# A decode-attention kernel that streams 162 MB: keys scored 16384 at a time, values in 64-column tiles, a row-form mixer, and a new division of the load buffers

## The chip, the cores and the metric

The kernel runs on one core of one Trainium2 chip. The metric is the device time of one execution in microseconds (us), median over several runs. The runs of the kernel before agree within 0.2%.

The words used below: PE is the matrix engine, PEld its weight loads, DVE the vector engine, ACT the scalar engine, SP the engine that issues the loads. "The queue" is the one DMA queue on which SP issues every large load; it is worked off by 16 DMA engines in parallel. A DMA engine moves one row of a load, here mostly 32 KB, as one packet.

## The reference, cut to what matters

One token is decoded. Attention has 32 query heads on 4 key/value heads, 65536 cached positions of 128 elements; beside it stands a small gated mixer, and a sigmoid gate blends the two.

```python
# per kv head g: K, V are [65536, 128] bf16 (16.8 MB each); 8 query heads share them
q      = x @ wq                                   # wq  1024 x 4096   (8.4 MB)
p      = softmax(q @ K.T * 128**-0.5)
a      = concat_heads(p @ V) @ wo                 # wo  4096 x 1024   (8.4 MB)
z      = gelu(x @ w_in)                           # w_in 1024 x 3584  (7.3 MB)
b      = (z[:1792] * (w_sp * layernorm(z[1792:]) + b_sp)) @ w_out   # w_out (3.7 MB)
gate   = sigmoid((x * gate_w).sum())
out    = gate * a + (1 - gate) * b
```

Every byte is read once: 162 MB for hardly any arithmetic. All keys of a head must be scored before its values are used, because the maximum is taken first.

## The kernel before

A recorder notes each operation with what it reads and writes; each engine runs its own operations in the order in which they were recorded and waits on semaphores where an operand comes from another engine or a load. Loads are issued in one fixed order, and a load waits until the readers of the buffer that it overwrites are done. If that wait lasts longer than the loads already queued, the queue runs dry.

```python
NS, SLOT = 5, 16384            # ring of five slots, 128 partitions x 32 KB = 4 MB each

def k_piece(n, j):             # a quarter of 8192 keys
    P("DVE", lambda e: e.transpose(ktb(i).bitcast(F32), sl[:, 2048*j:2048*(j+1)].bitcast(F32)),
      r=[key], w=[("kt", i % NKTS)])                     # three buffers for transposed keys
    def f(e):
        for fe in range(4):
            ins = e.matmul(pf(sb), qpad[g % 2][:, o:o+128], vw(ktb(i), ...),   # 128 x 512, own weight load
                           start=(j == 0 and fe == 0), stop=(j == 3 and fe == 3))
    P("PE", f, r=[("qpad", g % 2), ("kt", i % NKTS)], w=[B(sb)])
    ...
def pv_piece(n):               # 8192 values: 16 matmuls, four column tiles of 32
    for b in range(16):
        cg = b % 4
        ins = e.matmul(pf(OB)[32*cg:32*(cg+1), :], ptsb(n)[:, 32*b:32*(b+1)], vw(sl, 128*b, [[2048,4],[1,128]]),
                       tile_position=(0, 32*cg), ...)
def win_piece(i):              # mixer in column form: 4 x 56 matmuls with one column each
    for k in range(2):
        for z in range(2*FC):
            ins = e.matmul(pf(MB)[:, z:z+1], vw(sl, c0, [[FC,128]]), xT[:, 2*i+k:2*i+k+1], ...)
# ... (softmax, mixer's small operations, output product cut)
```

## Time and profile before

| | before |
|---|---|
| median | 386.56 us (3 runs, 386.56 to 386.72) |
| span in the profile | 384.9 us |
| moved by the queue | 162.01 MB |
| PE, DVE busy | 61%, 55% |
| DMA engines busy with packets | 98.2% |

The lines below are from the page of the kernel before: span, busy time of the engines, the rate of the queue in 40 equal slices, the queue's total with its share of 16 engines' span, and the shares of the chain that ended last.

```profile
span 384.9 us, 3607 instructions
PE 233.6 (61%) x1547; PEld 86.2 (22%) x1547; DVE 211.6 (55%) x329; ACT 30.6 (8%) x71; POOL 2.1 (1%) x9
...
GB/s 331 436 433 440 430 424 437 429 435 433 427 433 426 427 433 429 433 432 436 433 429 436 424 429 436 429 431 430 433 433 431 433 430 429 434 433 422 421 418 169
...
q1 hardware_dynamic: 6200, 162.01, 98.2%
...
DMA 71%; PE 16%; DVE 11%; issue 0%; SPq 0%
```

The row counts a packet in the slice where it starts, so it wavers by some 10 GB/s without any idle time; only a clear drop outside the two ends would be time in which the queue had nothing to do, and before, there is none. The share of 98.2% says the same.

The costliest groups of the page of before (line, engine, operation, shapes, count | busy us, mean ns of one | idle before, and who ended it):

```profile
L472 PE MATMUL pb<-arena 128*128 128x512 bf16 x512 | 160.0, 457 | 93.6 <-DVE arena L464 91.7
L464 DVE STREAM_TRANSPOSE arena<-arena 128x1024 f32<-128x1024 f32 x128 | 151.4, 1217 | 75.3 <-DMA arena<-in_A_k_cache_dram 75.0
L472 PEld LDWEIGHTS pb<-arena 128*128 128x128 bf16 x512 | 46.7, 109 | 201.3 <-DVE arena L464 144.9
L516 PE MATMUL pb<-arena 128*32 128x512 bf16 x512 | 39.3, 441 | 20.6 <-DMA arena<-in_A_v_cache_dram 18.1
...
L558 PE MATMUL pb<-arena 128*128 128x1 bf16 x224 | 13.7, 198 | 0.0
```

Key matmuls wait for DVE's transposes, and those wait for the load of the keys (75 us): this chain of waits leads back to the queue.

### The profile page before, as it was taken

To read this page: it belongs to the slowest core of one execution; us is meant where nothing else is said; L and a number is where in the kernel's file an instruction comes from. 1 tells how busy PE (TensorE), PEld (TensorE's weight loads), DVE (VectorE), ACT (ScalarE), POOL (GpSimd) and SP (SyncE) were. 2 spreads that over 40 slices of the span, in tenths; PEclk is the share of its full clock that TensorE was granted. 3 is DMA by queue.
4 is the path that set the end of the run, shared out by engine and by line. 5 is a ranking of instruction groups with operands and counts; after the bars stand their busy time and mean duration, and the time that the engine had idled before them with its cause. 6 is when DMAs were issued, how large, how long until landed. Compare 5 with 4: busy or idle time off the path is not lost.

```text
span 384.9 us, 3607 instructions
## 1 busy us (share of the span) xinstructions
PE 233.6 (61%) x1547; PEld 86.2 (22%) x1547; DVE 211.6 (55%) x329; ACT 30.6 (8%) x71; POOL 2.1 (1%) x9
## 2 busy tenths in 40 slices
PE   0434888478776656563687574726983829533354
PEld 0111455423221111111222121212220202211121
DVE  4115454489967474655596656645974748511010
ACT  1000000100300000001010000000100000320000
POOL 2000000000000000000000000000000000000000
PEclk9985969569996969696889696956796979866655
DMA  8999999999999999999999999999999999999994
GB/s 331 436 433 440 430 424 437 429 435 433 427 433 426 427 433 429 433 432 436 433 429 436 424 429 436 429 431 430 433 433 431 433 430 429 434 433 422 421 418 169
DMA packets 6228, 162.24 MB, mean 422 GB/s; under 512 B 700, under 2 KB 708, under 8 KB 964
## 3 DMA queue, kind: packets, MB, share of 16 engines
q1 hardware_dynamic: 6200, 162.01, 98.2%
q8 instruction: 12, 0.20, 0.2%
q14 instruction: 4, 0.03, 0.0%
q10 hardware_dynamic: 12, 0.00, 0.0%
HBM read 162.01 MB, written 0.00 MB: 421 GB/s over the span
## 4 chain that ended last, share of the span: by engine, by line
DMA 71%; PE 16%; DVE 11%; issue 0%; SPq 0%
DMA arena<-in_A_k_cache_dram 59%; PE pb L472 11%; DMA arena<-in_A_v_cache_dram 10%; DVE arena L464 9%; DMA arena<-in_A_wo_dram 3%; PE pb L516 2%; PE pb L558 2%; DVE arena L485 1%; PE pb L650 1%; DVE arena L507 0%; DVE arena L533 0%; PE pb L538 0%; PE pb L528 0%; SPq L349 0%; PE pb L495 0%
## 5 line engine op out<-in xcount | busy, mean ns | idle before, releaser
L472 PE MATMUL pb<-arena 128*128 128x512 bf16 x512 | 160.0, 457 | 93.6 <-DVE arena L464 91.7
L464 DVE STREAM_TRANSPOSE arena<-arena 128x1024 f32<-128x1024 f32 x128 | 151.4, 1217 | 75.3 <-DMA arena<-in_A_k_cache_dram 75.0
L472 PEld LDWEIGHTS pb<-arena 128*128 128x128 bf16 x512 | 46.7, 109 | 201.3 <-DVE arena L464 144.9
L516 PE MATMUL pb<-arena 128*32 128x512 bf16 x512 | 39.3, 441 | 20.6 <-DMA arena<-in_A_v_cache_dram 18.1
L502 ACT ACTIVATE arena<-arena 128x512 bf16<-128x512 f32 x32 | 23.1, 720 | 224.0 <-DVE arena L507 171.1
L507 DVE STREAM_TRANSPOSE arena<-arena 128x512 bf16<-128x512 bf16 x32 | 21.6, 679 | 18.5 <-PE pb L516 18.5
L485 DVE TENSOR_SCALAR_CACHE_REDUCE arena<-pb 128x512 f32<-128x512 f32 x32 | 21.6, 674 | 8.1 <-PE pb L472 7.9
L516 PEld LDWEIGHTS pb<-arena 128*32 128x32 bf16 x512 | 12.8, 106 | 45.0 <-issue 37.1
L558 PEld LDWEIGHTS pb<-arena 128*128 128x128 bf16 x224 | 13.8, 161 | 0.4
L558 PE MATMUL pb<-arena 128*128 128x1 bf16 x224 | 13.7, 198 | 0.0
L650 PE MATMUL pb<-arena 128*1 128x256 bf16 x128 | 7.8, 410 | 6.3 <-DMA arena<-in_A_wo_dram 6.3
L530 DVE RECIPROCAL arena<-pb 128x1 f32<-128x1 f32 x4 | 0.7, 168 | 18.4 <-PE pb L528 18.4
L419 PE MATMUL pb<-arena 128*2 128x512 bf16 x64 | 6.8, 601 | 4.2 <-DMA arena<-in_A_wq_dram 4.2
L656 DVE TENSOR_TENSOR arena<-pb,arena 97x256 bf16<-97x256 f32 x1 | 0.4, 425 | 13.4 <-PE pb L650 13.4
L396 PE MATMUL pb<-arena 1*128 1x2 bf16 x1 | 0.2, 158 | 10.1 <-DMA arena<-in_B_b_sp_dram 10.1
L426 DVE CAST arena<-pb 98x512 bf16<-98x512 f32 x1 | 0.7, 692 | 10.2 <-PE pb L419 10.2
L502 ACT ACTIVATION_READ_ACCUMULATOR arena<-arena 128x1 f32 x32 | 6.0, 187 | 0.0
L650 PEld LDWEIGHTS pb<-arena 128*1 128x1 bf16 x128 | 3.4, 109 | 10.5 <-DMA arena<-in_A_wo_dram 7.6
L538 PE MATMUL pb<-arena 128*128 128x128 bf16 x16 | 1.8, 243 | 5.2 <-DVE arena L533 5.2
L573 ACT ACTIVATE arena<-arena 128x28 f32<-128x28 f32 x1 | 0.2, 227 | 55.8 <-DVE arena L572 55.8
L569 DVE COPY arena<-pb 128x28 f32<-128x28 f32 x1 | 0.2, 186 | 7.8 <-PE pb L558 7.8
L398 DVE COPY arena<-pb 128x2 f32<-128x2 f32 x1 | 0.2, 159 | 7.7 <-PE pb L396 7.7
(88 smaller groups left out, 50.4 us busy)
## 6 DMA issues: line engine op xcount, KB each, us to landing
arena<-in_A_k_cache_dram SPq DMA_DIRECT2D x16, 4096.0 KB, 30.9
arena<-in_A_v_cache_dram SPq DMA_DIRECT2D x16, 4096.0 KB, 36.4
arena<-in_A_wq_dram SPq DMA_DIRECT2D x2, 4096.0 KB, 17.2
arena<-in_B_w_in_dram SPq DMA_DIRECT2D x2, 3584.0 KB, 40.9
arena<-in_A_wo_dram SPq DMA_DIRECT2D x3, 2048.0 KB, 34.9
arena<-in_B_w_out_dram SPq DMA_DIRECT2D x1, 3584.0 KB, 34.4
arena<-in_A_wo_dram SPq DMA_DIRECT2D x1, 1024.0 KB, 23.1
arena<-in_A_wo_dram SPq DMA_DIRECT2D x2, 512.0 KB, 13.1
```

The lines of the kernel that those rows point to most:

```text
L419: ins = e.matmul(pf(OB)[32 * cg:32 * cg + 2, :], xw[:, 3 * c + 1 - s:3 * c + 3 - s], sl[:, WQ_N * k + 512 * (4 * s + cg):WQ_N * k + 512 * ...
L426: P("DVE", lambda e: e.tensor_copy(qsb[0:98, :], pf(OB)[0:98, :]), w=[("psb", 0), B(OB)])
L464: P("DVE", lambda e: e.transpose(ktb(i).bitcast(F32), sl[:, 2048 * j:2048 * (j + 1)].bitcast(F32)), r=[key], w=[("kt", i % NKTS)])
L472: ins = e.matmul(pf(sb), qpad[g % 2][:, o:o + 128], vw(ktb(i), 64 * f2 + ev, [[128, 16], [2, 32]]), start=(j == 0 and fe == 0), stop=(j == ...
L485: P("DVE", lambda e: e.tensor_scalar(scs(n), pf(sb), 0.0, None, op0=ALU.add, op1=ALU.max, accum_out=maxc[:, n:n + 1]), w=[("sc", n % NSC), ...
L502: P("ACT", lambda e: e.activation(psb(n), scs(n), ACTF.Exp, bias=gcol(g, K_NB), scale=SCALE, accum_out=lp[:, n:n + 1]), r=[("sc", n % NSC) ...
L507: P("DVE", lambda e: e.transpose(ptsb(n), psb(n)), r=[("psb", n % 2)], w=[("ptsb", n % 2)])
L516: ins = e.matmul(pf(OB)[32 * cg:32 * (cg + 1), :], ptsb(n)[:, 32 * b:32 * (b + 1)], vw(sl, 128 * b, [[2048, 4], [1, 128]]), start=(u == 0 ...
L530: P("DVE", lambda e: e.reciprocal(gcol(g, K_RL), pf(MB)[:, 0:1]), w=[("rl", g), B(MB)])
L538: ins = e.matmul(pf(MB)[:, 0:128], sel[:, 128 * c:128 * (c + 1)], osc[:, 128 * c:128 * (c + 1)], start=(c == 0), stop=(c == 3))
L558: ins = e.matmul(pf(MB)[:, z:z + 1], vw(sl, c0, [[FC, 128]]), xT[:, 2 * i + k:2 * i + k + 1], start=(i == 0 and k == 0 and z == 0), stop=( ...
L650: ins = e.matmul(pf(FB)[32 * q:32 * q + 1, 0:QW], ovec[:, 8 * i + c:8 * i + c + 1], sl[:, o:o + QW], start=(i == 0 and c == 0), stop=(i == ...
```

## The change

The intent is to feed PE in larger pieces. A query weight is loaded once and used for two PSUM banks, so 16384 keys are scored per step; values go through two column tiles of 64 with shared weights; the mixer's input product is turned so that x is the weight and w_in streams in rows of 448 columns. The 20 MB of load buffers are divided anew: three 4 MB slots for keys (and a few weights), and one 8 MB region for values, wq, w_in and most of wo (the last two value blocks go to key slots). The core of the diff, with cuts:

```diff
-    NS = 5
-    SLOT = 16384
+    SUB = 16384
+    KR = 3                       # key ring: 3 slots of 4 MB
+    NSUB = KR + 2                # and an 8 MB value region behind it
-    NKTS = 3
+    NKT = 2
 ...
+    def mm(e, loaded, *a, **kw):             # a matmul that reuses the weights already loaded
+        if not loaded:
+            return e.matmul(*a, **kw)
+        ...  dataclasses.replace(one, ..., ldweights=False)
 ... # order of the loads
+    load([("wq", 0)], rows(A_wq, 0, 8), VB)
+    load_k(0)
+    load_k(1)
+    load([("win", 0)], rows(B_w_in, 0, 8), VB)
+    load_k(2)
+    load_k(3)
+    load([("wout", 0)], rows(B_w_out, 0, 14), kring())
+    for i in range(6):
+        load_k(2 * i + 4)
+        load_v2(2 * i)                       # two value blocks, the whole region
+        load_k(2 * i + 5)
+    load_v2(12)
 ... # a load is cut into DMAs of one slot, each waiting only for the readers of its own part
+            for c in range(0, w, SUB):
+                m = min(SUB, w - c)
+                P("SP", ... e.dma_start(arena[:, o:o + m], src), w=[("slot", x) for x in grains(off + c, m)], ...)
 ... # key scoring
-                ins = e.matmul(pf(sb), qpad[g % 2][:, o:o + 128], vw(ktb(i), 64 * f2 + ev, [[128, 16], [2, 32]]), ...)
+                for b in range(2):
+                    ins = mm(e, b > 0, sc_ps(n)[:, 512 * b:512 * (b + 1)], qpad[:, o:o + 128],
+                                   vw(ktb(i), 2048 * b + 64 * f2 + ev, [[128, 16], [2, 32]]), ...)
 ... # values
+            for i in range(16):
+                b, t, cg = i // 8, 2 * (i % 8), i % 2
+                for h in range(2):
+                    ins = mm(e, h > 0, ob[64 * cg:64 * (cg + 1), 512 * h:512 * (h + 1)], ..., tile_position=(0, 64 * cg))
 ... # mixer
+            for c in range(KC):
+                for k in range(4):
+                    for s in range(2):
+                        ins = mm(e, s > 0, ob[32 * k:32 * k + 1, 512 * s:512 * s + FB4], xT[:, c:c + 1], sl[:, o:o + FB4],
+                                       tile_position=(0, 32 * k), ...)
 ... # the order at the start
+    k_step(0)
+    k_step(1, evac=0, own=True)
+    mixer_piece()
+    k_step(2)
+    k_step(3, evac=2)
+    wout_piece()
```

## The prediction

> **What bounds the kernel now.** The DMA queue. The slices row shows 424 to 440 GB/s in all slices but the first (331) and the last four (422, 421, 418, 169). The queue moved 162.01 MB; at 432 GB/s that is 375 us of the 384.9 us span. The Trainium skill, "DMA: Bandwidth & Descriptors", Specifications, puts the fabric ceiling at 435 GB/s; this trace agrees (about 431 held). The rest is about 3 us before data flows and, after the last weights land at 381.7 us (chain of waits), some PE and DVE work and the store. PE (233.6 us, 61%) and DVE (211.6 us, 55%) have slack. The chain is 71% DMA.
>
> **What the change does.** The bytes stay, in rows of 32 KB as before.
> - Keys: 512 matmuls stay, their 512 weight loads (46.7 us, mostly overlapped) become 256. 128 transposes of 1.22 us become 64 of an estimated 2.35; 32 evictions of 0.67 become 16 of about 1.25. Saves about 5 us of DVE.
> - Values: 512 matmuls stay, but two column tiles run side by side instead of four. Before, 16 took 1.01 us (timeline); I estimate 2 us per 16 warm, 3.4 cold: PE gains 30 us of work.
> - Mixer: 224 one-column matmuls (13.7 us) become 64 of 448 columns, about 7 us, plus 2.2 us of row copy and transpose on DVE.
> - Buffers: still 20 MB, but keys own three 4 MB slots and values one 8 MB region that isn't double buffered.
>
> None of the saved engine time lies on the critical path. The change can win almost nothing; it loses where the queue runs dry.
>
> **Where the queue could run dry** (estimates from the trace's durations; a 4 MB load takes 9.7 us).
> 1. The fifth key load reuses the slot of key block 2, whose transposes stand on DVE behind the mixer. w_in lands at about 59.4, its matmuls end at 67.5, copy and transpose take 2.2, the small operations 6.0 (70.7 to 76.7 before), and block 2's transposes, paced by a cold PE (0.39 to 0.43 us per matmul), end at about 87.5. The queue has drained by about 86.3. Gap 2.5 us, range 0 to 6.
> 2. Values 12-13 wait for the product of block 11, with only one 9.7 us key load between instead of two. Gap 1 us, range 0 to 4.
> In the steady state the products end some 14 us before the region is needed: no gap. The tail is the same.
>
> **Predicted: 388.8 us**, range 385.6 to 394.0. Faster by over 2%: 0.02 (it would need a DMA rate above 435). Within 2%: 0.88. Slower by over 2%: 0.10.
>
> **What would show each step.** Right: DMA about 71% or more of the chain; steady slices at 425 to 440 GB/s; one slice near 85 to 95 us down to 300 to 400, with the fifth key load's issue waiting for block 2's last transpose; perhaps a smaller dip near 320 us, waiting for a value product. Groups: transposes near 2.35 us, 256 key weight loads, value products 2 to 3.4 us per 16. The skill's "TensorE: Matmul & The Clock Gate", Part 1, has an idle PE at half rate; the trace agrees (16 key matmuls at 34 us took 6.28 us, later ones 0.26 each).
> Wrong: no dip at all (then about 386), or dips every 39 us.
>
> **What would make it wrong.** Two matmuls sharing a weight in one column tile may not overlap the other tile: products of 7 to 14 us per block, and gap 2 grows to 6 us. Key and value rows now stand 64 KB apart in HBM; if that lowers the rate by 1%, it costs 4 us.

## The result, and the profile after

| | before | after |
|---|---|---|
| median | 386.64 us (4 runs, 386.56 to 386.75) | 386.15 us (4 runs, 385.93 to 386.49) |
| ratio | | 0.9988, 95% interval 0.9974 to 1.0002 |
| span in the profile | 384.9 us | 384.5 us |

A ratio is the mean time of one kernel's fast runs over that of the other's in the same rounds, so it isn't quite the ratio of the medians quoted beside it. The change is within the noise of nothing: the predicted loss of 2.2 us (388.8 against 386.6) did not come.

The same lines of the page of after:

```profile
span 384.5 us, 2520 instructions
PE 236.3 (61%) x1367; PEld 57.8 (15%) x777; DVE 212.3 (55%) x229; ACT 25.8 (7%) x42; POOL 1.5 (0%) x8
...
GB/s 328 436 436 436 435 417 440 433 403 419 435 426 426 423 436 431 436 436 433 433 431 433 433 436 421 426 426 430 436 436 428 433 436 433 429 433 424 418 424 204
...
q1 hardware_dynamic: 6200, 162.01, 98.4%
...
DMA 63%; PE 18%; DVE 17%; SPq 1%; issue 1%; ACT 0%
```

The ninth slice (76.9 to 86.5 us) shows 403 and the tenth 419: the predicted dip is there, but shallow. The 417 of the sixth slice is no gap: the packet records have no idle time in it. Everywhere else the queue is as full as before. Three in ten of the instructions are gone (3607 to 2520), and it made no difference. The chain's DMA share fell from 71% to 63% although the queue is busy for 98.4% of the span, against 98.2%: more of the chain runs through DVE (17% against 11%) and PE (18% against 16%). The faster kernel of run 2 has only 55% DMA in it, so this share is no measure of how bound the kernel is.

The groups of after that answer to those of before:

```profile
L483 DVE STREAM_TRANSPOSE arena<-arena 128x2048 f32<-128x2048 f32 x64 | 145.2, 2292 | 81.9 <-DMA arena<-in_A_k_cache_dram 73.6
L253 PE MATMUL scp<-arena 128*128 128x512 bf16 x256 | 108.7, 425 | 85.4 <-DVE arena L483 62.0
L255 PE MATMUL scp<-arena 128*128 128x512 bf16 x256 | 107.7, 421 | 0.0
...
L253 PEld LDWEIGHTS scp<-arena 128*128 128x128 bf16 x256 | 26.9, 105 | 190.7 <-DVE arena L483 95.8
```

L253 and L255 are the first and second matmul of a shared weight; their spans overlap, so their busy times must not be added. Key weight loads went from 46.7 to 26.9 us and key transposes from 151.4 to 145.2 us, and DVE waits for the keys' load as long as before (73.6 against 75.0 us). Nothing of this reached the time. DVE's total didn't fall either (211.6 before, 212.3 after): the mixer's copy and transpose add 2.2 us, a second pass over each head's output 2.9 us and smaller operations about 3 us; the rest is overlap of neighbouring records, which the total counts once.

**Where the queue came closest to running dry.** First the timeline of DVE in after (start, duration, what, and in brackets the idle time before it with its releaser). L595 takes the mixer's sums out of PSUM, L625 is the mixer's last operation, L483 are the transposes of key block 2, which stand behind the mixer; the cut leaves out the mixer's small operations.

```profile
66.46 1.09 DVE L595 COPY arena<-obt 128x896 f32<-128x896 f32 x1 [10.27 <-PE obt L255]
67.58 1.11 DVE L597 STREAM_TRANSPOSE arena<-arena 128x896 f32<-128x896 f32 x1
...
74.47 0.23 DVE L625 SCALAR_TENSOR_TENSOR arena<-arena 128x14 bf16<-128x14 f32 x1
74.62 4.50 DVE L483 STREAM_TRANSPOSE arena<-arena 128x2048 f32<-128x2048 f32 x2
80.61 2.31 DVE L483 STREAM_TRANSPOSE arena<-arena 128x2048 f32<-128x2048 f32 x1 [1.50 <-PE scp L255]
83.58 4.50 DVE L483 STREAM_TRANSPOSE arena<-arena 128x2048 f32<-128x2048 f32 x2 [0.66 <-PE scp L255]
```

Block 2's last transpose is the first of the two that begin at 83.58, so it ends at about 85.9. The issue of the fifth key load follows at once, in the timeline of SP:

```profile
85.92 0.33 SPq L373 DMA_DIRECT2D arena<-in_A_k_cache_dram  x1
```

The packet records of the trace give the rest. The last packets of w_out end between 86.37 and 87.87 us, engine by engine, and the first packet of the fifth key load starts at 86.87. So the engines that were ahead stood idle for up to about a microsecond, and the hindmost not at all: 0.47 us averaged over the 16. The Trainium skill, "DMA: Bandwidth & Descriptors", Specifications, gives 0.6 us as the first-byte latency of a load issued from SP; here it is 0.62 us from the end of the issue (86.25) to the first packet.

**The packets right after such a gap are slow.** Packets of 32 KB take 1.220 us on average in the profile of before. The 17 slow ones just after the gap took 0.53 us more per engine in total, as the first ones of the whole program do (0.54 us in the first 10 us). So this gap cost its idle time and about half a microsecond to start again. Slow packets alone are no sign of a gap: the same profile has 27 of them between 36 and 49 us (0.25 us per engine) with no idle time of note.

### The profile page after: what moved, and what is told of

It is laid out like the page before. It is cut to its first block, busy times and chain, and to the rows that moved or that the text cites. A ratio compares the mean times of both kernels' runs of the same rounds, so it can differ in the third digit from the quotient of the medians.

```text
span 384.5 us, 2520 instructions
## 1 busy us (share of the span) xinstructions
PE 236.3 (61%) x1367; PEld 57.8 (15%) x777; DVE 212.3 (55%) x229; ACT 25.8 (7%) x42; POOL 1.5 (0%) x8
## 3 DMA queue, kind: packets, MB, share of 16 engines
q1 hardware_dynamic: 6200, 162.01, 98.4%
## 4 chain that ended last, share of the span: by engine, by line
DMA 63%; PE 18%; DVE 17%; SPq 1%; issue 1%; ACT 0%
DMA arena<-in_A_k_cache_dram 33%; DVE arena L483 11%; DMA arena<-in_A_v_cache_dram 8%; DMA arena<-in_B_w_in_dram 8%; DMA arena<-in_A_wo_dram 8%; DMA arena<-in_A_wq_dram 6%; PE obt L253 5%; PE obt L255 5%; PE scp L253 4%; PE scp L255 3%; SPq L373 1%; DVE arena L500 1%; DVE arena L521 1%; DVE arena L556 0%; DVE arena L471 0%
## 5 line engine op out<-in xcount | busy, mean ns | idle before, releaser
L483 DVE STREAM_TRANSPOSE arena<-arena 128x2048 f32<-128x2048 f32 x64 | 145.2, 2292 | 81.9 <-DMA arena<-in_A_k_cache_dram 73.6
L253 PE MATMUL scp<-arena 128*128 128x512 bf16 x256 | 108.7, 425 | 85.4 <-DVE arena L483 62.0
L255 PE MATMUL scp<-arena 128*128 128x512 bf16 x256 | 107.7, 421 | 0.0
L253 PE MATMUL obt<-arena 128*64 128x512 bf16 (+2 forms) x334 | 70.1, 445 | 31.5 <-DMA arena<-in_A_v_cache_dram 15.2
L255 PE MATMUL obt<-arena 128*64 128x512 bf16 (+2 forms) x334 | 69.7, 442 | 0.0
L253 PEld LDWEIGHTS scp<-arena 128*128 128x128 bf16 x256 | 26.9, 105 | 190.7 <-DVE arena L483 95.8
L253 PEld LDWEIGHTS obt<-arena 128*64 128x64 bf16 (+1 forms) x334 | 20.8, 118 | 92.7 <-issue 88.1
L516 ACT ACTIVATE arena<-arena 128x1024 bf16<-128x1024 f32 x16 | 18.4, 1148 | 223.3 <-DVE arena L512 112.5
L500 DVE TENSOR_SCALAR_CACHE_REDUCE arena<-scp 128x1024 f32<-128x1024 f32 x16 | 19.3, 1205 | 9.3 <-PE scp L255 9.3
L521 DVE STREAM_TRANSPOSE arena<-arena 128x1024 bf16<-128x1024 bf16 x16 | 19.4, 1213 | 8.1 <-PE obt L255 5.5
L706 PE MATMUL fbt<-arena 128*1 128x256 bf16 x128 | 7.0, 384 | 4.2 <-DMA arena<-in_A_wo_dram 4.1
L595 DVE COPY arena<-obt 128x896 f32<-128x896 f32 x1 | 1.1, 1091 | 10.3 <-PE obt L255 10.3
L706 PEld LDWEIGHTS fbt<-arena 128*1 128x1 bf16 x128 | 3.4, 106 | 7.5 <-DMA arena<-in_A_wo_dram 4.6
```

What stands on the lines that cost most here:

```text
L253: return e.matmul(*a, **kw)
L255: one = e.matmul(*a, **kw).ins
L483: P("DVE", lambda e: e.transpose(ktb(i).bitcast(F32), sl[:, 4096 * p:4096 * (p + 1)].bitcast(F32)), r=keys[2 * p:2 * p + 2], w=[("kt", i % ...
L500: P("DVE", lambda e: e.tensor_scalar(scs(n), sc_ps(n), 0.0, None, op0=ALU.add, op1=ALU.max, accum_out=maxc[:, n:n + 1]), w=[("sc", n % NSC ...
L516: P("ACT", lambda e: e.activation(psb, scs(n), ACTF.Exp, bias=gcol(n // NP, K_NB), scale=SCALE, accum_out=lp[:, n:n + 1]), r=[("sc", n % N ...
L521: P("DVE", lambda e: e.transpose(ptsb(n), psb), r=["psb"], w=[("ptsb", n % 2)])
```

## The experiments

The averages of idle and slow time that follow come from the packet records of each profile, between 78 and 98 us: idle is time with fewer than 16 packets in flight, divided over the 16 engines; slow is the excess of packets over 1.3 us above 1.220 us, also per engine.

### 1. The changed kernel again, as yardstick

> The changed kernel again, as the yardstick for the three runs beside it and as a second profile of it. Expected 386.0 to 386.5 us, 0.1% under the kernel before. In the packets of the DMA queue the only gap in the middle is again at 86 to 88 us, about 0.5 us averaged over the 16 engines; the engines' last packets end within about 2 to 4 us of each other, and this spread at the end differs from run to run.

Measured: 386.04 us (6 runs, 385.34 to 387.53), ratio to the kernel before 0.9987 (0.9971 to 1.0002). In its profile the fifth key load was issued at 84.22 us, not 85.92, with 0.12 us idle and 0.29 us slow.

```profile
84.22 0.33 SPq L373 DMA_DIRECT2D arena<-in_A_k_cache_dram  x1
```

What follows: the gap is there in both profiles, but at a quarter of the idle time that was expected. It is too small to be seen in the row of rates, whose ninth and tenth slices show 429 and 425:

```profile
GB/s 327 435 435 435 434 434 435 432 429 425 434 432 425 435 422 420 432 435 435 435 430 432 435 432 434 432 435 429 429 429 427 422 432 435 432 432 434 417 421 137
```

PE's granted clock differs too. From 60 to 68 us, where the mixer's matmuls run, the view by windows gives 0.63 in the first profile and 0.79 in this one, and block 2's first transpose begins 1.2 us sooner (73.41 against 74.62). From 77 to 86 us it gives 0.67 and 0.79, and DVE's transposes of block 2 waited for PE in both. The third profile (run 11) has 0.79, 0.81 and an issue at 83.94. That the clock sets the size of the gap is likely, but no run isolates it. Its range of times (2.2 us) is much wider than that of the kernel before (0.3 us).

### 2. Key block 2 before the mixer

```diff
     k_step(1, evac=0, own=True)
-    mixer_piece()
-    k_step(2)
+    k_step(2)
+    mixer_piece()
     k_step(3, evac=2)
```

> Key block 2 is scored before the mixer, so its slot is free some 5 us before the queue drains. Theory A (the gap exists, but it is only about 0.5 us because the mixer and block 2 end 1.6 us sooner than predicted): the fifth key load is issued before 82 us, the dip at 86 to 88 us disappears, and the time falls by 0.0 to 0.5 us. Theory B (the gap costs about 2.5 us as predicted, and the change gained as much elsewhere): the time falls by 2 to 3 us, to about 383.7.

Measured: 385.41 us (5 runs, 385.19 to 385.53), ratio 0.9969 (0.9957 to 0.9981). The issue moved to 80.51 us:

```profile
80.51 0.33 SPq L373 DMA_DIRECT2D arena<-in_A_k_cache_dram  x1
```

Idle and slow time are both 0.00. What follows: the gap was real, and it was small. Theory A said 0.0 to 0.5 us, and the median fell by 0.63; theory B's 2 to 3 us is ruled out. The intervals of the two ratios overlap, so this pair alone doesn't settle the time; runs 11 and 12 repeat it.

### 3 and 4. The same issue made later on purpose

```diff
     mixer_piece()
+    for i in range(2):   # 6 in the second run
+        P("DVE", ... e.transpose(af("SC", 1024, 1024 * d), af("SC", 1024, 1024 * s)), r=[("sc", s)], w=[("sc", d)])
+    for j, d in enumerate((2, 3)):
+        P("DVE", ... e.tensor_copy(col(62 + j), af("SC", 1, 1024 * d)), r=[("sc", d)], w=["delay%d" % j])
     k_step(2)
```

> Two more transposes of 128x1024 (and two tiny copies) on DVE between mixer and block 2, about 2.7 us: the fifth key load is issued at about 88.6 us instead of 85.9, the size that the prediction had in mind. Theory A: the queue has a gap of about 3 us per engine on average and the time rises by 1.7 to 2.8 us, to 388 to 389, which is what was predicted. Theory C (a gap at this place costs nothing, because the loads catch up later or the end is limited by something else): within 0.4 us of the changed kernel.

> Six such transposes, about 7.5 us: issue at about 93.5 us. Theory A: the time rises by 6.5 to 7.5 us, to 392.5 to 394, one for one with the delay beyond the half microsecond of gap already there. Theory C: no change, or far less than the delay.

Measured: 387.81 us (5 runs, 387.27 to 387.94), ratio 1.0028 (1.0016 to 1.0040), and 393.31 us (4 runs, 391.92 to 393.57), ratio 1.0166 (1.0153 to 1.0179). All four kernels:

| kernel | fifth key load issued | idle | slow | sum | median | above kernel of run 2 |
|---|---|---|---|---|---|---|
| block 2 first (run 2) | 80.51 | 0.00 | 0.00 | 0.00 | 385.41 | |
| changed (run 1) | 84.22 | 0.12 | 0.29 | 0.41 | 386.04 | 0.63 |
| two more transposes | 87.14 | 2.02 | 0.53 | 2.55 | 387.81 | 2.40 |
| six more transposes | 92.44 | 7.24 | 0.51 | 7.75 | 393.31 | 7.90 |

The last two columns agree within 0.25 us. For the smallest gap that is partly luck, because the gap is read from one execution and the time is a median: the profiled executions themselves took 385.41, 387.13, 387.27 and 393.22 us, so that of the changed kernel lay 1.72 us above that of run 2 with a gap of only 0.41. (Its end differed too, see run 12.) The two larger gaps were made on purpose and stand clear of this. Their issues came 1.1 to 1.5 us before the expected 88.6 and 93.5 us, because the chain ended earlier than in the first profile (84.22 against 85.92), and so the first of them fell a little short of the expected 388 to 389 us.

In the view by windows, the lines of 84 to 88 us (first the stretch, then the busy times of PE, PEld, DVE, ACT and POOL, the clock, the DMA share and GB/s), of the changed kernel's first profile:

```profile
84.00:88.00 4.00, 3.18 (x14) 0.57 (x6) 4.00 (x2) 0.00 (x0) 0.00 (x0) 1.00 1.00 375
```

of block 2 before the mixer:

```profile
84.00:88.00 4.00, 1.58 (x36) 0.30 (x12) 2.29 (x3) 0.00 (x0) 0.00 (x0) 1.00 1.02 439
```

and of the kernel with two more transposes:

```profile
84.00:88.00 4.00, 3.33 (x16) 0.67 (x7) 3.42 (x3) 0.00 (x0) 0.00 (x0) 0.99 0.49 208
```

What follows: a gap in this queue is paid for in full and nothing later gives it back. Theory C falls. Had the issue come at the predicted 87.5 us, a good part of the predicted loss would have come true: two more transposes put it at 87.14, and that kernel is 1.2 us slower than the kernel before and 1.8 us slower than the changed one. Its idle time of 2.02 us also shows that the step from the time of issue to the size of the gap was about right.

### 5. The mixer in the old column form

```diff
-                for k in range(4):
-                    for s in range(2):
-                        ins = mm(e, s > 0, ob[32*k:32*k+1, ...], xT[:, c:c+1], sl[:, o:o+FB4], tile_position=(0, 32*k), ...)
+                for z in range(2 * FC):
+                    ins = e.matmul(mb[:, z:z + 1], vw(sl, c0, [[FC, 128]]), xT[:, c:c + 1], ...)
 ...
-        (row copy 128x896 and transpose)
+        P("DVE", lambda e: e.tensor_copy(zc, mb[:, 0:28]), w=[KZR, KZT, "mb"])
```

> The changed kernel with the mixer's input product in the old column form (224 one-column matmuls, 13.2 us in the profile of before, in place of 64 of 448 columns, 5.8 us; the row copy and transpose on DVE, 2.2 us, are gone again). Theory A (the queue's gap follows the time at which block 2's transposes end): that is some 5 us later, the fifth key load is issued at 89 to 91 us, the gap is 4 to 5 us and the time 390 to 391.5 us, so the mixer in row form is what the ring of three key slots needs. Theory E (the mixer's form does not matter, the prefetch of the other loads hides it): within 0.5 us of the changed kernel, about 386.

Measured: 391.53 us (4 runs, 391.10 to 392.10), ratio 1.0129 (1.0114 to 1.0144). The fifth key load is issued at 90.60 us; 5.31 us idle and 0.50 slow. The mixer's matmuls in its timeline, against the first and last of those in after, for which three lines of its timeline stand in the second fence:

```profile
60.40 13.57 PE L583 MATMUL mbt<-arena 128*128 128x1 bf16 x224 [5.64 <-DMA arena<-in_B_w_in_dram]
```

```profile
60.62 0.55 PE L253 MATMUL obt<-arena 128*1 128x448 bf16 x4 [5.70 <-DMA arena<-in_B_w_in_dram]
60.95 0.59 PE L255 MATMUL obt<-arena 128*1 128x448 bf16 x4
...
66.03 0.36 PE L255 MATMUL obt<-arena 128*1 128x448 bf16 x4
```

What follows: theory A holds, with gap and time just above the expected 4 to 5 and 390 to 391.5 us, and theory E falls. The row form takes 5.8 us in place of 13.6, and in this division of the buffers that is worth over 5 us of the whole. Here engine time stands right beside the critical path, because block 2's slot is wanted again as soon as w_out has been loaded. In the kernel before, with its ring of five, the same 224 matmuls left no dip in the row of rates.

### 6. One DMA for a whole value pair

```diff
-            for c in range(0, w, SUB):
-                m = min(SUB, w - c)
+            step = w if keys[0][0] == "v" else SUB
+            for c in range(0, w, step):
+                m = min(step, w - c)
```

> A value pair is loaded by one DMA of 8 MB with rows of 64 KB instead of two of 4 MB, so its load waits for the products of both blocks before it and each product waits for the whole pair: this is the dependency that the prediction had assumed. Theory A: values 12-13 are issued at the end of product 11, at about 320.5 us instead of 311.3, just when the queue drains (about 321), for a gap of 0 to 1 us there, and the time is 386.0 to 387.2; no gap in the steady state. If the packets become 64 KB and each packet has a fixed cost of about 9 ns (worked out from 1220 ns for 32 KB and 615 ns for 16 KB), up to 0.7 us of this comes back. Theory F (the value region is far from binding whatever its granularity): no gap near 320 us.

Measured: 389.51 us (4 runs, 389.33 to 389.60), ratio 1.0075 (1.0060 to 1.0091), so more than either theory said. The issue of values 12-13 in after, timeline of SP (four DMAs merged in one line, the first at 311.30):

```profile
311.30 6.86 SPq L373 DMA_DIRECT2D arena<-in_A_v_cache_dram  x4
```

and with the whole pair in one DMA, timeline of SP, then the view by windows around it:

```profile
321.86 1.28 SPq L374 DMA_DIRECT2D arena<-in_A_v_cache_dram  x3
```

```profile
318.00:320.00 2.00, 2.00 (x22) 0.54 (x10) 0.00 (x0) 0.00 (x0) 0.00 (x0) 1.00 0.65 279
320.00:322.00 2.00, 2.00 (x20) 0.59 (x8) 0.00 (x0) 0.00 (x0) 0.00 (x0) 1.00 0.19 82
```

The idle time there is 2.73 us and the slow packets after it cost 0.64. The queue began to drain at about 319, not at 321, and the two products ended later than estimated, because the first ran at half clock (5.06 us against 3.65 warm). Together that is 3.4 us, about as much as this kernel lies above the changed one in the other calls (386.0 to 386.2 us). The packets did become 64 KB and took 2.419 us at the median against twice 1.213 in the same profile, a gain of 0.3% or about 0.4 us in all. What follows: the prediction's second gap needs this dependency. In the changed kernel each 4 MB half waits only for the product of its own block, so the issue comes some ten microseconds earlier, and its packets show no idle time between 310 and 330 us.

### 7 and 8. Both kernels with a quarter of the key and value bytes

Their outputs are wrong, which doesn't matter for the times. Every engine keeps its instructions; only the loads shrink, so that the queue no longer hides the engines.

```diff
+                q = m // 4 if keys[0][0] in ("k", "v") else m
-                ... e.dma_start(arena[:, o:o + m], src), ...   # src[:, c:c + m]
+                ... e.dma_start(arena[:, o:o + q], src), ...   # src[:, c:c + q]
-          sl[:, 4096 * p:4096 * (p + 1)]                       # keys
+          sl[:, 0:4096]
-          vw(sl, 128 * (16 * b + t + h), [[4096, 4], [1, 128]])# values
+          vw(sl, 128 * ((t + h) % 8), [[1024, 4], [1, 128]])
```

(The edit of the kernel before is the same in its own terms.)

> Wrong results on purpose: the kernel before with only the first quarter of each key and value load brought in and read again for the rest, so that every engine has the same instructions and the queue moves about 61 MB (143 us) instead of 162. The engines bound it: DVE has 212 us of work and PE 234 us at a partly cold clock. Expected 225 to 270 us.

> Wrong results on purpose: the changed kernel with the same cut of the loads. Theory G (the change makes the engines' work cheaper, and the queue hides it): 3 to 10% faster than the cut kernel before, about 215 to 255 us. Theory H (fewer, larger pieces with one softmax buffer and two transpose buffers are coupled more tightly and the value products take more PE time, so the engines gain nothing either): equal to the cut kernel before or slower.

Measured: 286.76 us for the cut kernel before (4 runs, 286.18 to 287.57) and 308.93 us for the cut changed kernel (4 runs, 308.35 to 309.44). From the mean times of the two (286.82 and 308.91) the changed kernel is 7.7% slower. The kernel before was also above its expected range of 225 to 270.

The engines' lines of the two pages, before and then changed:

```profile
PE 209.1 (73%) x1547; PEld 79.3 (28%) x1547; DVE 211.8 (74%) x329; ACT 30.6 (11%) x71; POOL 2.1 (1%) x9
```

```profile
PE 215.3 (70%) x1367; PEld 53.5 (17%) x777; DVE 211.8 (69%) x229; ACT 25.8 (8%) x42; POOL 1.5 (0%) x8
```

What follows: theory G falls and theory H holds. DVE is busy for 211.8 us in both and PE for 209.1 and 215.3; so the larger pieces made neither of the two busy engines cheaper, and the schedule around them is worse. In the real kernel the queue hides this, as it would hide a gain.

### 9 and 10. What makes the cut changed kernel slower

With four column tiles of 32 for the values (wrong results, as above):

```diff
-            for i in range(16):
-                b, t, cg = i // 8, 2 * (i % 8), i % 2
-                for h in range(2):
-                    ins = mm(e, h > 0, ob[64 * cg:64 * (cg + 1), 512 * h:512 * (h + 1)], ..., tile_position=(0, 64 * cg))
+            for i in range(32):
+                cg = i % 4
+                ins = e.matmul(ob[32 * cg:32 * (cg + 1), 0:512], ptsb(n)[:, 32 * i:32 * (i + 1)], ..., tile_position=(0, 32 * cg))
```

> Wrong results on purpose: the changed kernel with quarter loads, and its value products as 32 matmuls of 32 columns in four column tiles instead of 64 columns in two. Theory J (with the queue out of the way, the changed kernel is slower than the old one because a pair of value products holds PE for 7.3 us instead of 4.2 and DVE, with two transpose buffers, has to wait): a block's product falls from 3.65 to about 1.9 us, 16 of them save 28 us of PE, and the time falls from 308.9 to 280 to 292 us, about the old kernel's 286.8. Theory K (the coupling is in the buffers and the order of the loads): it stays above 300.

With a third buffer for transposed keys:

```diff
-    NKT = 2
+    NKT = 3      # the third in a part of the ring that the quarter loads leave unused
```

> Wrong results on purpose: the changed kernel with quarter loads and a third buffer for transposed keys (placed in a part of the ring that the quarter loads leave unused). Theory J's second half (DVE waits because only two transposed pieces fit ahead of PE): DVE can run one piece of 2.25 us further ahead in each of some 7 product pairs, so 10 to 16 us come back: 292 to 299 us. Theory K': the wait is for the loads' order, no change from 308.9.

Measured: 286.70 us (4 runs, 286.45 to 287.58) with the 32-column tiles, the cut kernel before to within 0.1 us; and 302.75 us (4 runs, 301.60 to 303.36) with the third buffer, outside the 292 to 299 that was expected.

The lines below are DVE's waits by releaser (us in total, times, longest). The cut changed kernel (L547 opens the output of a head, L484 are the key transposes):

```profile
DVE arena L547 <- PE mbt L543: 17.3, 4, 5.9
...
DVE arena L484 <- PE scp L255: 12.5, 5, 3.2
```

With 32-column value tiles (the same two operations; lines are numbered two less from there on):

```profile
DVE arena L484 <- PE scp L255: 4.1, 4, 1.5
DVE arena L545 <- PE mbt L541: 3.4, 4, 2.3
```

With the third transpose buffer, the second of them:

```profile
DVE arena L484 <- PE scp L255: 3.1, 3, 1.0
```

What follows: theory J holds for the tiles. The 64-column tiles account for the whole loss of 22 us, together with the shared weights and the second PSUM bank, which the same edit takes back; these were not tested apart. The two waits shrink by 17.3 - 3.4 = 13.9 and 12.5 - 4.1 = 8.4 us, 22.3 together. That this is the loss to a tenth is partly luck, because other waits changed as well (the last output's wait for PE grew from 9.8 to 15.0 us). A pair of value products holds PE (twice about 3.65 us at full clock; before, the same 32768 values took four times 1.05 us), and both the next head's output and the next key transposes stand behind it. The third buffer removes only the wait of the transposes (12.5 to 3.1) and leaves the output's, and another wait of DVE for key matmuls gives 3.0 us back (L501, 9.3 to 12.3 us). I had expected 10 to 16 us from the buffer, and 6.2 came.

### 11 and 12. The better order, once more

> The changed kernel once more, beside the next run: 385.9 to 386.3 us.

> Key block 2 before the mixer, repeated to see whether its lead over the changed kernel holds. Theory A (it removes a gap of 0.1 to 0.5 us per engine): 0.2 to 0.7 us below the changed kernel of the same call, and 0.2 to 0.35% below the kernel before. If the first lead was chance: equal to the changed kernel.

Measured: the changed kernel 386.19 us (5 runs, 385.11 to 386.62), ratio 0.9982 (0.9969 to 0.9996); block 2 first 385.17 us (5 runs, 384.97 to 385.35), ratio 0.9962 (0.9949 to 0.9974). The lead is 1.0 us by the medians, above the 0.2 to 0.7 us that were expected.

What follows: the reordered kernel is the fastest of those with right results, 0.3 to 0.4% under the kernel before on two chips, which is clear of the noise and still far within 2%. Its lead over the changed kernel is small beside the latter's spread (the intervals of the ratios overlap), but in 8 of 11 executions the changed kernel was slower than the slowest of the reordered one's 10. The gap and its slow start explain about 0.4 of its 1.0 us here (0.18 idle and 0.23 slow in this profile of the changed kernel). The rest is at the end. In the two profiles of the reordered kernel the last packet ended at 379.94 and 379.72 us, in the three of the changed kernel at 380.93, 381.75 and 381.22, and in the kernel before at 381.24; the first of the 16 engines to finish did so 1.9 to 2.3 us before the last in the reordered kernel, 2.1 to 4.0 in the changed one and 3.4 in the kernel before. These ranges touch, and in the kernels of runs 3 to 6 it was 1.7 to 2.1 us, so a close end isn't peculiar to the reordered kernel. Why the engines end closer together in some executions stays open.

## Why the prediction was right or wrong

It called "within 2%" the likeliest class, and rightly. It forecast 388.8 us, a loss of 2.2; there was none. (Its two gaps add up to 3.5 us; it doesn't say how 2.2 comes of them.)

- **"The DMA queue bounds the kernel, and none of the saved engine time lies on the critical path."** Right. 20 us fewer of key weight loads and 6 us fewer of transposes moved nothing. The 5 us that DVE was to save came in its larger pieces and mostly went into its other work. But "saved" was too kind: with the queue out of the way (runs 7 to 10) the changed kernel is 7.7% slower, because of the value tiles.
- **"Gap 2.5 us" at the fifth key load: the step that failed, in its size.** Place and mechanism were right (runs 2 to 5). The mis-sized term is the time at which block 2's transposes end. The chain was summed to end at 87.5 us; it ended at 85.9, 84.2 and 83.9 us in three profiles, with 0.47, 0.12 and 0.18 us of idle queue in place of 2.5. The mixer's matmuls were put at 7 us and took 5.8, four of them running side by side in the trace (the prediction doesn't say how it came to 7). They were done at 66.4 instead of 67.5, and the rest of the chain gave back another half microsecond (in the first profile; more in the others). The time at which the queue drains, 86.3, was right to a tenth for the first engine; the last drained 1.5 us later. A difference of two sums of nearly 90 us, each good to about 2%, was forecast as 2.5; an error of 1.6 in one of them took most of it. What was left out altogether, the slow start after a gap (0.53, 0.29 and 0.23 us), is as large as the gap itself.
- **"Values 12-13 wait for the product of block 11", gap 1 us: the step that failed, in its dependency.** The diff cuts a load into DMAs of 4 MB, and each waits only for its own part's readers. The first half waits for block 10. Run 6 built the dependency that I had assumed, and then the gap is 2.7 us.
- **"In the steady state: no gap", "the tail is the same", "Key and value rows now stand 64 KB apart".** Right, and the last did no harm. No gap in the steady state, and packets of 32 KB took 1.222 us on average, against 1.220 before.
- **Marks in the profile.** Right: idle time of the queue at 86 to 88 us and nowhere else in the middle; 256 weight loads; transposes at 2.29 us for 2.35; value products at 1.8 us per 16 warm for 2. Wrong: the dip's depth (403 and 419 in its slices, not 300 to 400, and nothing to be seen in the row of the second profile), and a chain of 71% DMA or more (63%). For the half rate of an idle PE the prediction's two figures show a factor of 1.5 only; the starts of single key matmuls in the same trace show 1.9: they are 0.427 us apart from 34 us on and 0.22 us from the fourteenth on.
- **The remaining -0.4 us.** By the gap alone the changed kernel should be 0.4 to 1.0 us slower than the kernel before (idle and slow time of its three profiles), and it is as fast or 0.1 to 0.2% faster. The spread of the 16 engines at the end differs by as much from profile to profile. This isn't settled.

## What to carry to other kernels

When a queue is busy for 98% of the span, judge a change by one question: at which load does the buffer come free later than the queue drains? Follow the dependencies of each DMA as it is issued, not of the logical load, and count a gap as its idle time plus the slow start after it, here about half a microsecond. A gap that is the difference of two long sums should be forecast as a range from nothing, with most of the weight on its small side; and a saving or a loss of engine time that the queue hides can be measured by shrinking the loads alone.

## What the Trainium skill lacked or had wrong

- "DMA: Bandwidth & Descriptors" has no word on a queue that starts again after running dry: here the first packets of 32 KB, normally 1.220 us, took about 0.5 us per engine longer in total (0.53, 0.53, 0.51 and 0.50 us after four gaps of 0.5, 2.0, 7.2 and 5.3 us; 0.23, 0.29 and, in the run with whole value pairs, 0.72 after gaps of under 0.2 us).
- The same page's Specifications give 0.6 us to the first byte from SP, which agrees if one counts from the end of the issue (0.62 us); from its start it was 0.95 us. They give about 27 GiB/s per engine; here 32 KB packets run at 26.9 GB/s (25.0 GiB/s), 430 GB/s for 16, and packets of 64 KB gain 0.3%.
- The same page, in the table that calls engines 7 and 15 usually slower, has no figure for how far the 16 engines drift apart over a long stream: the first to finish ended 1.9 to 4.0 us before the last in the profiles of before, after and the reordered kernel. (The packet records name no engine, so whether it is those two can't be said.)
- "TensorE: Matmul & The Clock Gate", Part 3, has matmuls start strictly in program order. In the row-form mixer each column tile gets two matmuls in a row, yet the trace shows the first ones of all four tiles starting within 15 ns, and the four second ones 0.33 us later: 64 matmuls of 448 columns took 5.8 us.
